# Scales of the MLP weights in four groups, fewer weight tiles asked for in the first units, and four instead of eight float32 units

## The chip, the core and the metric

The kernel runs on one core of one Trainium2 chip. The metric is device time in microseconds (us) of one execution. The five engines of the core have a queue each and run their instructions in the order of that queue: PE (TensorE, matmuls; PEld is its weight load), DVE (VectorE), ACT (ScalarE), POOL (GpSimd) and SP (SyncE, which here issues all DMAs).

## What is computed

Attention in which a query sees only the keys of its own cluster, and behind it an MLP with a squared ReLU:

```python
q_assign = argmax(q_n @ c_n.T); k_assign = argmax(k_n @ c_n.T)     # 16 clusters a head
scores = where(q_assign[:, None] == k_assign[None, :], scale * q @ k.T, -1e9)
attn = exp(scores - max(scores)); attn /= sum(attn) + 1e-9
x = (attn @ v)                                                     # heads side by side: 3072 x 512
h = x @ w_in                                                       # 512 x 2048
g = s * relu(h) ** 2 + b
out = g @ w_out                                                    # 2048 x 512
```

There are 4 batches, 8 heads, 768 positions and a head dimension of 64. The two weight matrices are float64, so a load brings two 32-bit words for each of their elements; the other large inputs are float32.

## The kernel before, in words

**Units.** The attention is cut into 192 units: a batch, one third of its rows (a chunk of 256), a pair of heads, one of two row tiles, one of the two heads. `scores` (L464) makes a unit's 128 x 768 scores on PE into one of two PSUM tiles, `maxima` (L473) takes the row maxima on DVE, `exps` (L480, L483) the exponentials P on ACT. Then P is to be transposed, and there are two ways. The first RAW = 8 units keep P in float32: `low` turns it on PE into the PSUM tile `turned` (L503), DVE and ACT each copy half of it out (helper line L121 for DVE and POOL, L119 for ACT), and `values` multiplies in float32 (L520). The others go in two halves: `high` rounds P to float16 (a copy, on POOL up to unit 18, then on DVE for odd and ACT for even units up to unit 36, then on ACT), POOL subtracts it from P (`low`, L506), SP issues a DMA transpose of both halves (L508), and `values` uses three float16 matmuls for each key tile (L525 to L527). `values` comes five units behind `scores`. `finish_x` collects four units into a slice of x.

**MLP.** From unit LAG = 21 on, each unit is accompanied by one of 192 MLP steps: for a chunk of 256 rows (12 of them) one of the 16 slices of 128 hidden features. `mlp_in` (L583), `mlp_relu` (L590 to L593), POOL's low half (L598), `mlp_out` (L610), which sums over the 16 slices in the PSUM tile `acc` (of which there is one), and an eviction on DVE (L618) at the chunk's end. `mlp_start` (L568 to L574) makes a chunk's scales.

**Weights.** The 32 weight tiles (16 of `w_in`, 16 of `w_out`) stay in SBUF. `weights()` is a generator that for each tile issues its load into one of three `stage` buffers, two tiles later rebuilds a float32 from the two words (`rebase` on ACT, L203; `narrow` on DVE, L207 and L208), and one tile after that takes part in a bound (`bound`: an Abs pass on ACT, L215 and L217; for `w_in` also a sum over rows on PE, L220, and a maximum on DVE, L221). With the last tile `finish_w_in` and `finish_w_out` make one scale for all of `w_in` and one for all of `w_out` (L242 to L257, some 16 small DVE instructions). Only then `wsplit(ft)`, one slice in each unit from 17 to 32, can split the weights into float16 halves (L265 on ACT, L267 on DVE). A split goes into a tile of the pool `w`, which has 33 tiles, so that all but the first use the place of a tile that has just been split. `column_sums` (L275, L278) makes the bias term at the first chunk's end.

**What sets the order.** The main loop asks the generators for one unit after the other: `some(wgen, 2)` at its end asks for two weight tiles in each unit, `background()` moves on the preparation of the coming queries, keys and values (`prep_q`, `prep_k`, `prep_v`, whose start for batch 1 is in START). The framework's scheduler then decides how the instructions of neighbouring units follow each other in each engine's queue; what it wrote is shown under the change.

Of the kernel before, what the change touches and what calls it, by code (L numbers as in the profile page):

```python
# [26 lines left out]
def tile_cluster_attention_mlp(ctx, tc, q, k, v, cent, w_in, w_out, s_in, b_in, out):  # L27
# [18 lines left out]
    RAW = 8  # L46
# [60 lines left out]
    ones = const([P, P], BF16, "ones")  # L107
    G.memset(ones, 1.0)
    ident = const([P, P], F32, "ident")
# [4 lines left out]
    ones16 = const([P, P], F16, "ones16")  # L114
    G.memset(ones16, 1.0)
# [52 lines left out]
    def weight_tile(name):  # L168
        return cp.tile([P, KT, P], F32, tag="w", name=name, bufs=2 * NF + 1)
    w1 = const([P, NF], F32, "w1")  # L170
    l1 = const([P, NF], F32, "l1")
    glob = const([P, 12], F32, "glob")
# [28 lines left out]
    def rebase(d):  # L201
        hw = d["st"][:, :, :, 1].bitcast(F32)
        A.activation(d["w"], hw, AF.Prelu, scale=2.0 ** -112, alpha=-(2.0 ** 32))  # L203

    def narrow(d):
        c = d["w"].bitcast(I32)
        V.tensor_scalar(c, c, 3, None, op0=ALU.logical_shift_left)  # L207
        V.scalar_tensor_tensor(c.bitcast(U32), d["st"][:, :, :, 0].bitcast(U32), 29, c.bitcast(U32),  # L208
                               op0=ALU.logical_shift_right, op1=ALU.bitwise_or)

    def bound(d):
        w, p, ft = d["w"], d["p"], d["ft"]
        wa = sb.tile([P, KT, P], BF16, tag="wab", name=f"wab_{p}", bufs=2)
        if p % 2:
            A.activation(wa, w, AF.Abs, accum_out=l1[:, ft : ft + 1])  # L215
        else:
            A.activation(wa, w, AF.Abs)  # L217
            pw = ps_h.tile([P, 512], F32, tag="h", name=f"pw_{ft}")
            for t in range(KT):
                nc.tensor.matmul(pw[:, :P], ones, wa[:, t, :], start=(t == 0), stop=(t == KT - 1))  # L220
            V.tensor_reduce(w1[:, ft : ft + 1], pw[:, :P], axis=AX.X, op=ALU.max)  # L221
        if ft == NF - 1:
            (finish_w_out if p % 2 else finish_w_in)()
# [3 lines left out]
    def weights():  # L227
        live = {}
        for i in range(2 * NF + 3):
            if 0 <= i - 3:  # L230
                bound(live[i - 3])
# [9 lines left out]
    def finish_w_in():  # L241
        V.tensor_reduce(glob[:, 0:1], w1, axis=AX.X, op=ALU.max)  # L242
        V.tensor_scalar(glob[:, 0:1], glob[:, 0:1], 1.02, None, op0=ALU.mult)
        floor2(V, glob[:, 1:2], glob[:, 0:1])
        inverse2(V, glob[:, 2:3], glob[:, 1:2], 0)
        V.tensor_scalar(glob[:, 2:3], glob[:, 2:3], 2.0 ** 13, None, op0=ALU.mult)
        V.tensor_scalar(glob[:, 1:2], glob[:, 1:2], 2.0 ** -7, None, op0=ALU.mult)

    def finish_w_out():
        lc = columns(1, "w")  # L250
        V.tensor_reduce(lc, l1, axis=AX.X, op=ALU.max)
        allmax(glob[:, 4:5], lc, "w")
        floor2(V, glob[:, 4:5], glob[:, 4:5])
        inverse2(V, glob[:, 5:6], glob[:, 4:5], 0)
        V.tensor_scalar(glob[:, 5:6], glob[:, 5:6], 2.0 ** 13, None, op0=ALU.mult)
        V.tensor_scalar(glob[:, 4:5], glob[:, 4:5], 2.0 ** -13, None, op0=ALU.mult)
        V.tensor_tensor(glob[:, 6:7], sv, glob[:, 4:5], op=ALU.mult)  # L257

    def wsplit(ft):
        while narrowed[0] < 2 * NF:  # L260
            next(wgen)
        made = []
        for w, f in ((wi[ft], glob[:, 2:3]), (wo[ft], glob[:, 5:6])):
# [507 lines left out]
```

## Time and profile before

| | |
|---|---|
| median of three runs | 953.16 us (952.39 to 954.72) |
| profiled execution: device time | 953.86 us |
| profiled execution: span from the first to the last instruction | 952.2 us |
| PE busy | 828.6 us (87%) |
| ACT busy | 711.0 us (75%) |
| DVE busy | 626.1 us (66%) |
| POOL busy | 573.0 us (60%) |

How to read it: the profile is of one execution. An engine's busy time is the time in which one of its instructions ran. A row of a group of instructions gives line, engine, operation, output and input with shapes, then the count, behind the first bar the busy time and the mean duration in ns, behind the second the engine's idle time just ahead of them and what ended it. In a row of a stage (from:to in us from the span's start) the numbers are the stage's length, each engine's busy time with its count of instructions, PE's granted clock as a share of full speed, the busy share of the DMA engines (it can pass 1 where transfers overlap) and GB/s. In a timeline row the first number is the start, the second the duration in us.

### The profile page before, as it was taken

What the parts mean: (1) busy time and instruction counts of PE and PEld (TensorE: products, weight loads), DVE (VectorE), ACT (ScalarE), POOL (GpSimd) and SP (SyncE); (2) the same over time, 40 slices, a digit from 0 to 9 for tenths busy, and PEclk for the clock granted to TensorE, in tenths of its full rate; (3) what the DMA queues carried; (4) which work ended last, traced back from release to release, by engine and by line L of the source; (5) the groups of instructions that cost most, each with busy time, mean ns of one, the idle gap of its engine ahead of it and who ended that gap; (6) DMA issues with size and microseconds to landing.
All of it is one profiled execution on the core that took longest, in us unless ns stands there. A gap on an engine that the chain in (4) does not pass through costs nothing. (4 is left out here: it accounts for less than half of the span.)

```text
span 952.2 us, 22467 instructions
## 1 busy us (share of the span) xinstructions
PE 828.6 (87%) x8625; PEld 579.4 (61%) x8625; DVE 626.1 (66%) x1400; ACT 711.0 (75%) x1390; POOL 573.0 (60%) x596
## 2 busy tenths in 40 slices
PE   0668446988999989999899999999999999999997
PEld 0457324555666667766566666766666766767764
DVE  7797988999677657767865757668666466463100
ACT  4477656887688778987787877978787888789443
POOL 3012545677578566866767758667776765676321
PEclk9965556999999999999999999999999999999999
DMA  6888974876887796968689969758877757777100
GB/s 182 227 215 234 235 179 92 197 151 114 174 167 154 170 201 122 186 147 181 139 165 177 184 142 181 149 130 189 156 153 170 145 116 152 138 165 133 33 23 22
DMA packets 450300, 147.36 MB, mean 155 GB/s; under 512 B 417937, under 2 KB 446609, under 8 KB 450193
## 3 DMA queue, kind: packets, MB, share of 16 engines
q1 hardware_dynamic: 450192, 145.93, 72.2%
q8 instruction: 67, 1.10, 0.5%
q14 instruction: 41, 0.33, 0.1%
HBM read 35.69 MB, written 6.29 MB: 44 GB/s over the span
## 5 line engine op out<-in xcount | busy, mean ns | idle before, releaser
L506 POOL TENSOR_TENSOR ph<-p,ph 128x768 f16<-128x768 f32 x184 | 312.2, 1697 | 123.7 <-ACT ph L119 76.2
L583 PE MATMUL h<-x,wis 128*128 128x256 f16 x2304 | 287.6, 274 | 9.6 <-ACT r L590 8.0
L610 PE MATMUL acc<-wos,g 128*128 128x512 f16 x1152 | 292.6, 379 | 3.2 <-POOL g L598 2.8
L583 PEld LDWEIGHTS <-wis 128*128 128x128 f16 x2304 | 222.2, 98 | 59.5 <-issue 11.3
L598 POOL TENSOR_TENSOR g<-r,g 128x256 f16<-128x256 f32 x192 | 136.6, 713 | 101.7 <-ACT r L593 97.1
L473 DVE TENSOR_REDUCE ssm<-sc 128x1 f32<-128x768 f32 x192 | 181.5, 951 | 24.4 <-PE sc L464 23.6
L483 ACT ACTIVATE p<-sc,ssm,qsm 128x768 f32<-128x768 f32 x192 | 187.7, 978 | 3.4 <-DMA PT<-ph 1.0
L610 PEld LDWEIGHTS <-g 128*128 128x128 f16 x1152 | 103.6, 97 | 87.8 <-POOL g L598 5.7
L480 ACT ACTIVATE ssm<-ssm,lift,qsm 128x1 f32<-128x1 f32 x192 | 73.1, 381 | 92.5 <-DVE ssm L473 91.7
L119 ACT ACTIVATE ph<-p 128x768 f16<-128x768 f32 x164 | 136.1, 830 | 5.8 <-DMA PT<-ph 4.3
L590 ACT ACTIVATE r<-h,cf 128x256 f32<-128x256 f32 x192 | 89.1, 464 | 56.9 <-PE h L583 49.6
L525 PE MATMUL px<-vh,PT 128*128 128x65 f16 x1104 | 120.4, 197 | 12.9 <-DVE xs L537 6.8
L464 PE MATMUL sc<-KA,QA 128*128 128x384 f16 x384 | 99.9, 343 | 26.4 <-ACT p L483 23.4
L526 PE MATMUL px<-vl,PT 128*128 128x64 f16 x1104 | 120.3, 194 | 0.0
L527 PE MATMUL px<-vh,PT 128*128 128x65 f16 x1104 | 120.0, 195 | 0.0
L525 PEld LDWEIGHTS <-PT 128*128 128x128 f16 x1104 | 103.6, 98 | 23.1 <-issue 14.4
L526 PEld LDWEIGHTS <-PT 128*128 128x128 f16 x1104 | 103.3, 100 | 13.2 <-issue 5.1
L464 PE MATMUL sc<-KB,QB 128*128 128x384 f16 x384 | 100.1, 345 | 7.0 <-DMA QB<-qb 7.0
L527 PEld LDWEIGHTS <-PT 128*128 128x128 f16 x1104 | 103.5, 98 | 2.7
L592 ACT ACTIVATE g<-r 128x256 f16<-128x256 f32 x192 | 79.3, 413 | 4.0
L593 ACT ACTIVATE r<-r 128x256 f32<-128x256 f32 x192 | 78.8, 411 | 3.3
L464 PEld LDWEIGHTS <-QA 128*128 128x128 f16 x384 | 35.9, 101 | 54.9 <-issue 29.2
(156 smaller groups left out, 1032.3 us busy)
## 6 DMA issues: line engine op xcount, KB each, us to landing
wst<-in_moe_w_in_dram SPq DMA_DIRECT2D x16, 512.0 KB, 4.5
wst<-in_moe_w_out_dram SPq DMA_DIRECT2D x16, 512.0 KB, 4.5
kn<-in_k_dram SPq DMA_DIRECT2D x16, 384.0 KB, 4.1
qn<-in_q_dram SPq DMA_DIRECT2D x24, 256.0 KB, 3.5
vn<-in_v_dram SPq DMA_DIRECT2D x16, 384.0 KB, 4.1
out_dram<-o SPq DMA_DIRECT2D x12, 512.0 KB, 3.8
PT<-ph SPq DMA_TRANSPOSE x184, 3.5
x<-xn SPq DMA_TRANSPOSE x48, 2.5
```

The source lines that it names most:

```text
L119: A.activation(dst, src, AF.Copy)
L464: last_score[0] = nc.tensor.matmul(sc[:, e, :HALF], X[:, col, :], y[:, h * S + e * HALF : h * S + (e + 1) * HALF], start=st, stop=not st)
L473: last_max[0] = V.tensor_reduce(SM[i // 4][:, 0, j : j + 1], U[i]["sc"], axis=AX.XY, op=ALU.max, negate=True)
L483: last_exp[0] = A.activation(p.rearrange("p (a b) -> p a b", a=2), u["sc"], AF.Exp, bias=bi, scale=u["scale"], **total)
L506: G.tensor_tensor(u["ph"][:, 1, :], u["p"], u["ph"][:, 0, :], op=ALU.subtract)
L525: nc.tensor.matmul(o1, PT[:, kt, :], vh[:, h, kt, : D + 1], start=(kt == 0), stop=False)
L526: nc.tensor.matmul(o, PT[:, kt, :], vl[:, h, kt, :], start=False, stop=False)
L527: nc.tensor.matmul(o1, PT[:, T + kt, :], vh[:, h, kt, : D + 1], start=False, stop=(kt == T - 1))
L583: nc.tensor.matmul(ph[:, :CW], WSP[ft][0][:, wl, kt, :], XS[(b, c, kt)][:, :, xl, :], start=(i == 0), stop=(i == len(terms) - 1))
L590: A.activation(r, ph[:, :CW], AF.Relu, scale=MS[(b, c)][0])
L598: G.tensor_tensor(g[:, 1, :], r, g[:, 0, :], op=ALU.subtract)
L610: nc.tensor.matmul(acc[:, t, :], g[:, gl, rows], WSP[ft][1][:, wl, :], start=(ft == 0 and gl + wl == 0), stop=(ft == NF - 1 and gl == 1))
```

## The change

1. *Groups.* The 16 slices form four groups of four, each with scales of its own (`finish_group`), made as soon as the group's eight tiles are there. The bound is another one: the sums of squares of each column, as the diagonal of a product of the tile with itself on PE (the upper half of each float32 read as bfloat16), four tiles to a PSUM bank and one maximum on DVE for the four; the Abs pass is gone. `wsplit` waits for its group only. In the first chunk each group has its own `mlp_start` and its own accumulation, which DVE scales and adds up; the later chunks go on with one accumulation over all 16 slices, with a factor for each group. The column sums are made by group.
2. *Narrowing.* The shift of the rebuilt word goes into DVE's one remaining instruction (L211 in the new numbering); the low word is brought into place by a second ACT instruction in `rebase`.
3. *Rate.* No weight tile is asked for in units 0 to 3, one in each unit from 4 to 19, two from 20 on. The pool of weight tiles has 35.
4. *Units.* RAW is 4: units 4 to 7 go in two halves. POOL makes the float16 copy up to unit 30.
5. Batch 1's preparation starts at other units, `prep_v(0)` is moved on once more in unit 2, and two constant tiles are made later or not at all.

```diff
-    RAW = 8
+    RAW = 4
...
-        return cp.tile([P, KT, P], F32, tag="w", name=name, bufs=2 * NF + 1)
+        return cp.tile([P, KT, P], F32, tag="w", name=name, bufs=2 * NF + 3)
+    GROUP = 4
+    NG = NF // GROUP
...
     def rebase(d):
         hw = d["st"][:, :, :, 1].bitcast(F32)
         A.activation(d["w"], hw, AF.Prelu, scale=2.0 ** -112, alpha=-(2.0 ** 32))
+        A.activation(d["st"][:, :, :, 0], d["st"][:, :, :, 0].bitcast(U32), AF.Copy, scale=0.9375 * 2.0 ** -29, bias=-0.03125)
 
     def narrow(d):
         c = d["w"].bitcast(I32)
-        V.tensor_scalar(c, c, 3, None, op0=ALU.logical_shift_left)
-        V.scalar_tensor_tensor(c.bitcast(U32), d["st"][:, :, :, 0].bitcast(U32), 29, c.bitcast(U32),
-                               op0=ALU.logical_shift_right, op1=ALU.bitwise_or)
+        V.scalar_tensor_tensor(c.bitcast(U32), c.bitcast(U32), 3, d["st"][:, :, :, 0].bitcast(U32),
+                               op0=ALU.logical_shift_left, op1=ALU.bitwise_or)
...
+    def bound(pairs):
+        pw = ps_h.tile([P, 512], F32, tag="h", name=f"pw_{pairs[0][0]['ft']}")
+        for j, d in enumerate(sum(pairs, [])):
+            wa = d["w"].bitcast(BF16).rearrange("p a (f z) -> p a f z", z=2)[:, :, :, 1]
+            for t in range(KT):
+                nc.tensor.matmul(pw[:, j * P : (j + 1) * P], wa[:, t, :], wa[:, t, :], start=(t == 0), stop=(t == KT - 1))
+        ft = pairs[0][0]["ft"]
+        V.tensor_reduce(wsq[:, ft : ft + 2, :], pw.rearrange("p (f e q) -> p f e q", e=2, q=P), axis=AX.X, op=ALU.max)
+        if (ft + 2) % GROUP == 0:
+            finish_group(ft // GROUP)
...
     def wsplit(ft):
-        while narrowed[0] < 2 * NF:
-            next(wgen)
+        k = ft // GROUP
+        while narrowed[0] < 2 * GROUP * (k + 1):
+            next(wgen, None)
...
-    START = {b: [48 * b + x for x in ((-26, -25, -23, -20) if b == 1 else (-40, -38, -32, -28))] for b in range(1, B)}
+    START = {b: [48 * b + x for x in ((-24, -20, -22, -14) if b == 1 else (-40, -38, -32, -28))] for b in range(1, B)}
...
-        copy(G if i < LAG - 2 else V if i < LAG + NF and i % 2 else A, u["ph"][:, 0, :], u["p"])
+        copy(G if i < LAG + 10 else V if i < LAG + NF and i % 2 else A, u["ph"][:, 0, :], u["p"])
...
+        first = b + c == 0
+        span = GROUP if first else NF
+        k = ft // GROUP
+        if ft % span == 0:
+            MS[(b, c)][2] = ps_a.tile([P, CT, DM], F32, tag="acc", name=f"acc_{n}_{ft}")
...
+                if k == 0:
+                    V.tensor_scalar(o[:, t, :], acc[:, t, :], e, None, op0=ALU.mult)
+                else:
+                    V.scalar_tensor_tensor(o[:, t, :], acc[:, t, :], e, o[:, t, :], op0=ALU.mult, op1=ALU.add)
...
-        some(wgen, 2)
+        some(wgen, 0 if i < 4 else 1 if i < 20 else 2)
```

How the queues change, at three places. DVE before, from the maximum of unit 10 on; `wi` and `wo` are weight tiles, `wst` the loaded words, `pw` the bound's PSUM tile:

```order
L473 TENSOR_REDUCE ssm_864<-sc_975 128x1
L207 TENSOR_SCALAR wi_740<-wi_740 128x512
L68 TENSOR_SCALAR qsm_1_0_829<-qsm_1_0_829 128x2
L221 TENSOR_REDUCE w_128<-pw_774 128x1
L208 SCALAR_TENSOR_TENSOR wi_740<-wst_741,wi_740 128x512
L69 TENSOR_SCALAR qsm_1_0_829<-qsm_1_0_829 128x2
L207 TENSOR_SCALAR wo_783<-wo_783 128x512
L70 TENSOR_SCALAR qsm_1_0_829<-qsm_1_0_829 128x2
L208 SCALAR_TENSOR_TENSOR wo_783<-wst_784,wo_783 128x512
```

DVE in the changed kernel, from the maximum of unit 11 on:

```order
L493 TENSOR_REDUCE ssm_721<-sc_845 128x1
L553 TENSOR_SCALAR ssm_553<-px_859 128x2
L554 RECIPROCAL ssm_553<-ssm_553 128x2
L557 TENSOR_TENSOR xs_796<-px_859,ssm_553 128x128
L105 TENSOR_REDUCE xm_686<-xs_796 128x1
L211 SCALAR_TENSOR_TENSOR wo_740<-wo_740,wst_741 128x512
L221 TENSOR_REDUCE wsq<-pw_906 128x4
L493 TENSOR_REDUCE ssm_965<-sc_958 128x1
```

Of several tiles and two instructions a tile between two maxima one instruction is left, and a maximum over four tiles at once. Ahead of the maximum of unit 21 the changed row holds 19 of the 32 narrowings (three of them ahead of unit 0), the row before all 32.

The second place is DVE at units 26 to 28. Before, `vm` and `qsm` being the next values' and queries' preparation:

```order
L473 TENSOR_REDUCE ssm_1825<-sc_1867 128x1
L98 TENSOR_REDUCE qsm_2_0_1797<-am_q_2_0_1852 128x2
L473 TENSOR_REDUCE ssm_1825<-sc_1968 128x1
L267 SCALAR_TENSOR_TENSOR wos_1964<-wo_783,glob,wos_1964 128x512
L68 TENSOR_SCALAR qsm_2_0_1797<-qsm_2_0_1797 128x2
L101 TENSOR_REDUCE vm_1803<-vn_0_1804 128x1
L69 TENSOR_SCALAR qsm_2_0_1797<-qsm_2_0_1797 128x2
```

The changed kernel there, `gl` and `gsq` being a group's scales and `amb_w` their way to PE:

```order
L493 TENSOR_REDUCE ssm_1827<-sc_2014 128x1
L246 TENSOR_REDUCE amb_w_1780<-wsq 128x2
L282 SCALAR_TENSOR_TENSOR wos_1860<-wo_1090,gl,wos_1860 128x512
L282 SCALAR_TENSOR_TENSOR wis_1867<-wi_1174,gl,wis_1867 128x512
L211 SCALAR_TENSOR_TENSOR wo_1759<-wo_1759,wst_1760 128x512
L102 TENSOR_REDUCE gsq<-am_w_1782 128x2
L248 TENSOR_SCALAR gl<-gsq 128x1
L249 TENSOR_SCALAR gl<-gsq 128x1
L252 TENSOR_SCALAR gl<-gl 128x1 x2
L253 TENSOR_SCALAR gl<-gl 128x1 x2
L60 TENSOR_SCALAR gl<-gl 128x1
```

Narrowings and a group's chain of scales now stand between the splits and the maxima of units 21 to 31.

The third place is SP's queue in the units around 8. Before, loads of weight tiles nearly alone:

```order
L85 DMA wst_784<-in_moe_w_out_dram 128x1024
L85 DMA wst_792<-in_moe_w_in_dram 128x4x256
L85 DMA wst_849<-in_moe_w_out_dram 128x1024
L85 DMA wst_857<-in_moe_w_in_dram 128x4x256
L85 DMA wst_901<-in_moe_w_out_dram 128x1024
L85 DMA wst_909<-in_moe_w_in_dram 128x4x256
L508 DMA_TRANSPOSE PT_923<-ph_916 128x12x128
```

The changed kernel, one load for each transpose of P:

```order
L528 DMA_TRANSPOSE PT_660<-ph_653 128x12x128
L89 DMA wst_712<-in_moe_w_in_dram 128x4x256
L528 DMA_TRANSPOSE PT_727<-ph_719 128x12x128
L89 DMA wst_741<-in_moe_w_out_dram 128x1024
L528 DMA_TRANSPOSE PT_755<-ph_748 128x12x128
L89 DMA wst_816<-in_moe_w_in_dram 128x4x256
```

The transposes of units 4 to 8 have taken places between the loads, and the later loads have moved back past the transposes of later units.

More of the change, by code (lines that the diff above doesn't have):

```diff
@@ L106, in tile_cluster_attention_mlp @@
         G.memset(rev[:, c : c + 1], float(C - c))
-    ones = const([P, P], BF16, "ones")
-    G.memset(ones, 1.0)
-    ident = const([P, P], F32, "ident")
+    ident = sb.tile([P, P], F32, tag="g", name="ident", bufs=4)
     G.memset(ident, 1.0)
@@ L229, in weights @@
         for i in range(2 * NF + 3):
-            if 0 <= i - 3:
-                bound(live[i - 3])
+            p = i - 3
+            if p >= 0 and p % 4 == 3:
+                bound([[live[p - 3], live[p - 2]], [live[p - 1], live[p]]])
+            if p >= 0:
                 narrowed[0] += 1
@@ L602, in mlp_out @@
         n = f"{b}_{c}"
-        if ft == 0:
-            MS[(b, c)][2] = ps_a.tile([P, CT, DM], F32, tag="acc", name=f"acc_{n}")
+        first = b + c == 0
+        span = GROUP if first else NF
+        k = ft // GROUP
+        if ft % span == 0:
+            MS[(b, c)][2] = ps_a.tile([P, CT, DM], F32, tag="acc", name=f"acc_{n}_{ft}")
         acc = MS[(b, c)][2]
@@ L608, in mlp_out @@
             rows = slice(t * P, t * P + P)
-            for gl, wl in ((0, 0), (0, 1), (1, 0)):
-                nc.tensor.matmul(acc[:, t, :], g[:, gl, rows], WSP[ft][1][:, wl, :],
-                                 start=(ft == 0 and gl + wl == 0), stop=(ft == NF - 1 and gl == 1))
-        if ft == NF - 1:
-            _, e, acc = MS.pop((b, c))
-            o = sb.tile([P, CT, DM], F32, tag="stage", name=f"o_{n}", bufs=3)
-            if b + c == 0:
+            for gi, wl in ((0, 0), (0, 1), (1, 0)):
+                nc.tensor.matmul(acc[:, t, :], g[:, gi, rows], WSP[ft][1][:, wl, :],
+                                 start=(ft % span == 0 and gi + wl == 0), stop=(ft % span == span - 1 and gi == 1))
+        if ft % span < span - 1:
+            return
+        e = MS[(b, c)][1][:, k : k + 1] if first else MS[(b, c)][1][:, 0:1]
+        if k == 0 or not first:
+            MS[(b, c)].append(sb.tile([P, CT, DM], F32, tag="stage", name=f"o_{n}", bufs=3))
+        o = MS[(b, c)][3]
+        if first:
+            if ft == NF - 1:
                 column_sums()
             for t in range(CT):
+                if k == 0:
+                    V.tensor_scalar(o[:, t, :], acc[:, t, :], e, None, op0=ALU.mult)
+                else:
+                    V.scalar_tensor_tensor(o[:, t, :], acc[:, t, :], e, o[:, t, :], op0=ALU.mult, op1=ALU.add)
+                if ft == NF - 1:
+                    V.tensor_tensor(o[:, t, :], o[:, t, :], bias[0], op=ALU.add)
+        else:
+            for t in range(CT):
                 V.scalar_tensor_tensor(o[:, t, :], acc[:, t, :], e, bias[0], op0=ALU.mult, op1=ALU.add)
+        if ft == NF - 1:
+            MS.pop((b, c))
             nc.sync.dma_start(out[b * S : (b + 1) * S].rearrange("(p t) e -> p t e", t=T)[:, c * CT : (c + 1) * CT, :], o)
@@ L674, in prepare @@
                 run(first_k[3])
-                some(first_v, 1)
+                some(first_v, 2)
             if k == 3:
```

116 lines of the change are left out of this document (64 added, 52 removed).

## The prediction

> **What bounds the kernel now.** I read the page first: the span and the forty slices.
>
> ```profile
> span 952.2 us, 22467 instructions
> PE   0668446988999989999899999999999999999997
> DVE  7797988999677657767865757668666466463100
> PEclk9965556999999999999999999999999999999999
> DMA  6888974876887796968689969758877757777100
> ```
>
> From the tenth slice on (about 235 us) PE is full in almost every slice. Before it PE is half empty, its clock is at 5 tenths for a while, and DVE and the DMA engines carry the high digits. The change edits only things that happen before that point, so I cut the span at the row maxima of certain units (L473 on DVE, one per unit): unit 0 begins at 34.85 us, unit 8 at 70.84, unit 21 at 149.54, unit 32 at 210.66 and unit 42 at 262.22; the last exponential is at 878. Each engine's busy time by stage:
>
> ```profile
> core 0: us, PE busy (x) PEld busy (x) DVE busy (x) ACT busy (x) POOL busy (x), PEclk, DMA share, GB/s
> 34.85:70.84 35.99, 26.18 (x188) 20.16 (x187) 31.02 (x69) 26.02 (x54) 4.29 (x6) 0.77 0.90 239
> 70.84:149.54 78.70, 46.97 (x342) 33.32 (x339) 66.68 (x137) 49.77 (x97) 35.37 (x30) 0.59 0.80 200
> 149.54:210.66 61.12, 50.35 (x528) 34.42 (x529) 55.59 (x104) 48.00 (x92) 39.37 (x34) 0.89 0.77 159
> 210.66:262.22 51.56, 46.31 (x472) 30.16 (x470) 41.09 (x95) 36.56 (x68) 32.65 (x30) 1.00 0.73 147
> 262.22:878.00 615.78, 583.54 (x6472) 410.94 (x6470) 396.95 (x887) 502.89 (x979) 431.12 (x425) 1.00 0.78 158
> ```
>
> I call the first two rows stage A (units 0 to 20, 114.7 us), the third B (units 21 to 31, 61.1), the fourth C, the fifth D. In D, PE is busy 583.5 of 615.8 us (95%): nothing but PE work matters there, and the change leaves D's work alone. In B, DVE is busy 55.6 of 61.1 (91%): it is the bound. In A, DVE is busy 97.7 of 114.7 (85%) with the DMA engines close behind. So the question is what moves out of A, what moves into B, and at what rate each gives or takes.
>
> **What leaves A.** These are the DVE groups of stage A, by shape:
>
> ```profile
> L473 DVE TENSOR_REDUCE ssm<-sc 128x1 f32<-128x768 f32 x21 | 19.9, 950 | 4.0 <-PE sc L464 4.0
> L208 DVE SCALAR_TENSOR_TENSOR wi<-wst,wi 128x512 uint32<-128x512 uint32 x14 | 14.7, 1048 | 0.1
> L208 DVE SCALAR_TENSOR_TENSOR wo<-wst,wo 128x512 uint32<-128x512 uint32 x15 | 12.7, 850 | 0.1
> L207 DVE TENSOR_SCALAR wi<-wi 128x512 int32<-128x512 int32 x14 | 9.6, 689 | 3.7 <-ACT wi L203 3.7
> L207 DVE TENSOR_SCALAR wo<-wo 128x512 int32<-128x512 int32 x15 | 6.9, 457 | 4.0 <-ACT wo L203 4.0
> L121 DVE COPY PT<-turned 128x384 f32<-128x384 f32 x8 | 4.4, 547 | 1.8 <-PE turned L503 1.8
> L221 DVE TENSOR_REDUCE w<-pw 128x1 f32<-128x128 f32 x15 | 4.2, 281 | 1.4 <-PE pw L220 1.4
> L101 DVE TENSOR_REDUCE amb_q<-qn 128x2 bf16<-128x512 f32 x2 | 1.4, 686 | 1.3 <-DMA qn<-in_q_dram 1.3
> ```
>
> Twenty-nine of the 32 weight tiles are narrowed in A now. In the changed program's written-out row on DVE 16 of these come ahead of the maximum of unit 21, and 13 behind it. So, on DVE in A:
> - L208: 27.4 us for 29 tiles, 16 stay: -12.3. The new instruction has the same two inputs and shape, so I keep its price.
> - L207 is folded into it: -16.5.
> - L221: -4.2, and in its place four reductions of 128x512, which I price as the one of the same length, amb_q, at 0.69: +2.7.
> - Four copies of turned P, at 0.547: -2.2.
> - The single scale chain, some 16 small instructions, becomes the first group's, 24 small ones. The small ones are in this excerpt of DVE's timeline:
>
> ```profile
> 132.10 0.15 DVE L243 TENSOR_SCALAR glob<-glob 128x1 f32<-128x1 f32 x1
> 132.84 0.15 DVE L246 TENSOR_SCALAR glob<-glob 128x1 f32<-128x1 f32 x1
> 132.91 0.14 DVE L247 TENSOR_SCALAR glob<-glob 128x1 f32<-128x1 f32 x1
> ```
>
> They take 0.15 each (0.07 from start to start where the next doesn't wait for the one before): 24 x 0.15 - 2.9 = +0.7.
>
> Sum on DVE: -31.8, from 97.7 to 65.9 us. At A's present 85% that would be 77.5 us, but another cover comes up first, the DMA engines. They are busy 0.90 x 36.0 + 0.80 x 78.7 = 95.4 us of A. One weight tile costs 1.92 us of them: 0.524 MB at 298 GB/s is 1.76, times the share of 1.09 in this window:
>
> ```profile
> 36.00:48.00 12.00, 10.32 (x77) 8.00 (x78) 7.99 (x16) 8.52 (x20) 0.59 (x1) 1.00 1.09 298
> ```
>
> Thirteen tiles fewer are -25.0. The four units that leave the float32 way add four transposes of 0.393 MB; at D's 158 GB/s for a share of 0.78, one is 1.94: +7.8. That leaves 78.2 us. I take 84 us for A (93% of that share; DVE at 78%), so **A: -31**. The lower end is 78 (the share goes to 1 and beyond, as in the row above): -37. The upper end is 98, if only half of DVE's relief is turned into time: -17.
>
> What also eases A: ACT and PE.
>
> ```profile
> L203 ACT ACTIVATE wo<-wst 128x512 f32<-128x512 f32 x15 | 9.9, 661 | 7.0 <-DMA wst<-in_moe_w_out_dram 7.0
> L215 ACT ACTIVATE wab<-wo 128x512 bf16<-128x512 f32 x15 | 9.4, 625 | 2.6 <-DVE wo L208 2.5
> L520 PE MATMUL px<-vn,PT 128*128 128x64 f32 x96 | 20.0, 386 | 0.0
> L503 PE MATMUL turned<-ident,p 128*128 128x128 f32 x48 | 12.3, 385 | 7.2 <-DVE PT L121 3.7 <-ACT p L483 2.1 <-ACT PT L119 1.3
> ```
>
> The Abs pass (0.625) goes and a conversion of the low words comes; its shape and stride are L203's, so 0.66: a wash per tile, never on the path at ACT's 66% in A. The exponentials stand behind L203 in ACT's queue, and L203 waits 7.0 us there for tiles that have just been asked for; with one tile per unit the tile has landed long before. The float32 way costs PE 4.0 us per unit (20.0 / 8 + 12.3 / 8), so four units fewer are 16 us of PE, in a stage where PE holds up the scores behind it. On the other side, POOL gets four casts and four subtractions:
>
> ```profile
> L506 POOL TENSOR_TENSOR ph<-p,ph 128x768 f16<-128x768 f32 x11 | 19.3, 1751 | 0.6
> L121 POOL CAST ph<-p 128x768 f16<-128x768 f32 x11 | 11.3, 1024 | 18.6 <-ACT p L483 16.6 <-issue 2.0
> ```
>
> That is 2.8 us for each pair, so POOL goes from 39.7 us to 51 of 84, no bound.
>
> **What enters B.** DVE's groups in B, and the eviction's row from C:
>
> ```profile
> L267 DVE SCALAR_TENSOR_TENSOR wis<-wi,glob,wis 128x512 f16<-128x512 f32 x11 | 12.9, 1168 | 0.7 <-ACT wis L265 0.7
> L267 DVE SCALAR_TENSOR_TENSOR wos<-wo,glob,wos 128x512 f16<-128x512 f32 x12 | 11.3, 943 | 1.4 <-ACT wos L265 1.3
> L473 DVE TENSOR_REDUCE ssm<-sc 128x1 f32<-128x768 f32 x11 | 10.4, 947 | 0.6 <-PE sc L464 0.5
> L121 DVE CAST ph<-p 128x768 f16<-128x768 f32 x6 | 3.8, 630 | 0.0
> L618 DVE SCALAR_TENSOR_TENSOR o<-acc,xm,bias 128x512 f32<-128x512 f32 x2 | 1.4, 746 | 0.0
> ```
>
> Thirteen narrowings at 0.95 (the mean of L208's 29): +12.3. Four reductions at 0.69: +2.7. Three chains of scales, 72 small instructions at 0.15: +10.8. Three more starts of the first MLP chunk, 21 small ones at 0.17: +3.5. Two group evictions of the accumulator, four at 0.75: +3.0. Six casts move to POOL: -3.8. Sum +28.5, from 55.6 to 84.1 us. B is DVE's already, so nothing hides this; the only give is DVE's idle 9%. Some of that closes, because ACT and DVE now pass one spare tile to and fro:
>
> ```profile
> ACT wis L265 <- DVE wos L267: 9.1, 5, 2.6
> ACT wos L265 <- DVE wis L267: 5.9, 7, 1.7
> ```
>
> With two tiles more, ACT's 15 us of waiting for L267 can run ahead. I take 95.5% for DVE: 84.1 / 0.955 = 88.1, **B: +27**. Lower end: narrowing at its undisturbed 0.68 (below) and small ones at 0.10: -7, so +20. Upper end: 91% as now and PE's slower clock (second rival): +39.
>
> The price of 0.95 holds POOL's interference, seen where both engines' rows stand together (start, duration):
>
> ```profile
> 121.79 1.63 POOL L506 TENSOR_TENSOR ph<-p,ph 128x768 f16<-128x768 f32 x1
> 121.82 2.15 DVE L208 SCALAR_TENSOR_TENSOR wi<-wst,wi 128x512 uint32<-128x512 uint32 x1
> ```
>
> The weight tile's own view gives L208's least, median and greatest duration in ns:
>
> ```profile
> L208 DVE SCALAR_TENSOR_TENSOR wi<-wst,wi x16: 676/692/2152, 26.4 to 127.1; 128x512 uint32<-128x512 uint32 x16
> ```
>
> L208's minimum is 0.68; started 0.03 us behind a POOL subtraction of 1.63, it took 2.15, about the two in a row. Eleven casts more on POOL in B (units 19 to 30 no longer use DVE or ACT for them) make this likelier. [...]
>
> **C to the end.** The first chunk's accumulator is now read in four parts and the column sums in four, each time with PE waiting for a DVE instruction of 0.75: four such waits in C, about 1.2 us each with the wait for DVE's turn, +5. The splits that C still does now are done in B, and C's PE is busy 46.3 of 51.6, so some of that idle time closes: -3. **C: +2** (-4 to +6). D and the tail keep their instructions: 0.
>
> Sum: -31 + 27 + 2 = -2 us against the profiled execution's 953.9 us, which lies 0.7 above the median of the three runs (953.2). So 951 for the median. DVE's total is nearly the same before and after (about -31.8 + 28.5 and a little in C): work is moved, not saved, and a gain needs A to shrink by more than B grows.
>
> **The rivals.**
> 1. *Faster.* A goes to its DMA floor of 78 us (-37) and B takes only its lower +20, since narrowing loses the instruction (L207) that POOL stretched to 689 ns in the mean against 457 for the other half, and ACT runs ahead. -37 + 20 + 2 = -15: 938. For it: A's idle times are waits of weights on DMA and of scores on float32 PE work, both of which go. Against it: the 12.3 us of narrowing meet POOL in B as well.
> 2. *Slower, PE's clock.* PE's granted clock follows its busy share in the stage rows: 60% busy has 0.59, 82% has 0.89, 90% has 1.00. B stretched to 88 us holds 50.4 us of PE plus some 6 for 64 squaring matmuls (four in 0.40 us at full clock, below): 64%, near A's. If the clock falls to 0.6, PE's 44.8 + 6 us at full clock become 85, as much as DVE's 84, and each then waits for the other in queue order: B at about 100, +39. -31 + 39 + 2 = +10: 963. It decides from a clock under 0.7 in B; above that PE has room. The matmuls priced here, from the timeline:
>
> ```profile
> 45.37 0.40 PE L220 MATMUL pw<-wab,ones 128*128 128x128 bf16 x4
> ```
>
> [...]
> 3. *Slower, A does not shrink.* The change's first aim fails: the transposes of units 4 to 7 and weight tiles queue behind each other on SP, which issues in order, and A stays at 98. -17 + 27 + 2 = +12: 965.
>
> **How the numbers follow.** Cancelling within a few us (944 to 958): 0.40, of which 0.17 under 950.3, 0.17 within, 0.06 above. Rival 1: 0.27. Rival 2: 0.25. Rival 3: 0.08. About 0.3% (2.9 us, 950.3 to 956.0) is what a measurement of this kernel can tell from no change. Faster: 0.17 + 0.27 = 0.44; same: 0.17, with 0.01 from the upper rivals' lower edge, 0.18; slower: 0.06 + 0.33 - 0.01 = 0.38. The range reaches from rival 1's 938 with 3 us of its own spread to rival 3's 965 with 3: 935 to 968; the likeliest case's own is 944 to 958.
>
> **What would show it.** The maximum of unit 21 near 119 us (A at 84), with the DMA share above 0.9 in A; the maximum of unit 32 near 207, with DVE busy over 90% between the two; PE full from there. Unit 21 before 115 and unit 32 before 200 is rival 1. A granted clock under 0.7 and PE busy over 85% between units 21 and 32 is rival 2. Unit 21 after 130 is rival 3. The forecast is wrong altogether if stage D's 615.8 us change by more than a few us, since I give no reason for that.

## The result: 3.4% slower, and where the profile after shows it

| | before | after |
|---|---|---|
| median, four runs each, on one chip by turns | 953.94 us (952.39 to 957.18) | 986.92 us (984.81 to 989.29) |
| ratio, 95% interval | | 1.0342 [1.0303, 1.0381] |
| profiled execution, span | 952.2 us | 986.2 us |

The forecast was 951 us, and its range ended at 968. These are the same rows of the page of after, and below them the stages cut at the same maxima (L493 on DVE now), with a stretch further on. One limit in the prediction is misnamed: counted by their records, the maximum that begins at 262.22 us in before is the 44th, so unit 43's and not unit 42's; in after the 44th begins at 283.31.

```profile
span 986.2 us, 22636 instructions
...
PE   0585566598998799999889889999889899999997
...
DVE  6767598999477666637746557656656556464100
...
PEclk9956579899999799999999999999999999999999
DMA  6869899579669896996799898979779778878300
```

The stages of after (columns as in the prediction):

```profile
35.65:76.41 40.76, 30.35 (x229) 23.57 (x228) 29.18 (x59) 20.20 (x36) 16.22 (x15) 0.75 0.82 165
76.41:135.85 59.44, 32.78 (x306) 21.18 (x306) 40.77 (x100) 36.34 (x63) 34.52 (x30) 0.63 0.93 205
135.85:221.60 85.75, 61.62 (x609) 40.93 (x609) 77.92 (x214) 63.21 (x121) 48.13 (x45) 0.88 0.81 189
...
308.00:333.00 25.00, 15.93 (x189) 10.05 (x186) 19.71 (x42) 14.56 (x24) 15.49 (x14) 0.74 0.84 170
```

Stage A went from 114.7 to 100.2 us (-14.5; forecast -31), B from 61.1 to 85.8 (+24.6; forecast +27), C, up to 283.31, from 51.6 to 61.7 (+10.1; forecast +2). The last exponential came at 878 before and at 911.9 now, so D went from 615.8 to 628.6 (+12.8; forecast 0). The last row above is a hole: around 320 us, far behind all weights, PE is busy 15.93 of 25 us and its clock falls to 0.74. The same stretch of before has none:

```profile
308.00:333.00 25.00, 24.07 (x271) 17.11 (x269) 15.98 (x40) 18.71 (x37) 15.12 (x15) 1.00 0.81 176
```

Stages cut by units hide one thing: MLP steps shift among them. A better ledger is PE's unused time. Busy time multiplied by the granted clock is PE's work, in us at full clock; the length of a stretch less this work is what PE left unused, by idling or by a low clock. It is summed over stretches of 5 us (192 such rows for before, 201 for after). "MLP step 40" is the start of that step's relu on ACT (345.1, 364.7 and, in the run with both mends told below, 354.4 us).

| PE time not used, us | before | after | both mends |
|---|---|---|---|
| up to unit 0 | 28.1 | 29.4 | 30.3 |
| A: units 0 to 20 | 66.8 | 58.7 | 55.3 |
| B: units 21 to 31 | 14.8 | 31.2 | 31.2 |
| unit 32 to MLP step 40 | 11.4 | 20.4 | 13.4 |
| MLP step 40 to the last exponential | 26.2 | 39.3 | 23.6 |
| tail | 5.8 | 6.0 | 6.3 |
| sum | 153.1 | 185.0 | 160.1 |
| span less sum: PE's work | 799.1 | 801.2 | 798.6 |

PE's work is nearly the same in sum (799 to 801 us): the float32 work that went has been made up by work that came, the squares among it. So a shorter A is worth only what it takes from PE's unused time, and that is 8 us, not 14.5. B loses 16 again, and 22 us are lost behind unit 32, where the forecast had 2.

The start of some MLP steps (their relu on ACT) shows the same as differences to before, in us; one_sum to before_shift160 are runs told below:

| MLP step (before at) | after | one_sum | align | one_align | before_shift160 |
|---|---|---|---|---|---|
| 8 (195.5) | +9.7 | +7.7 | +8.4 | +7.6 | +0.9 |
| 28 (295.0) | +0.5 | +10.6 | -0.7 | +4.9 | +4.3 |
| 32 (314.0) | +18.2 | +17.7 | +16.5 | +11.9 | +6.1 |
| 40 (345.1) | +19.5 | +15.8 | +16.9 | +9.2 | +6.4 |
| 88 (548.3) | +27.3 | +22.6 | +17.0 | +8.0 | +13.5 |
| 188 (936.1) | +33.8 | +24.1 | +15.6 | +6.0 | +18.3 |

At step 28 after stands level with before. That is not the whole state of the kernel: at step 8 it was 9.7 us behind, and its attention is 11 us behind at the maximum of unit 32 (221.60 against 210.66) and 21 us at the 44th (283.31 against 262.22). Behind step 28 come a step of 18 us and a drift of 14.

**The step.** DVE's timeline of after holds the four readings of the column sums (start, duration):

```profile
254.51 0.74 DVE L296 TENSOR_SCALAR bias<-pb,gl 128x512 f32<-128x512 f32 x1
...
258.80 0.75 DVE L298 SCALAR_TENSOR_TENSOR bias<-pb,gl,bias 128x512 f32<-128x512 f32 x1 [2.68 <-PE pb L293]
...
263.78 0.75 DVE L298 SCALAR_TENSOR_TENSOR bias<-pb,gl,bias 128x512 f32<-128x512 f32 x1 [3.37 <-PE pb L293]
...
268.11 0.75 DVE L298 SCALAR_TENSOR_TENSOR bias<-pb,gl,bias 128x512 f32<-128x512 f32 x1 [3.58 <-PE pb L293]
```

ACT's timeline there has the exponentials of units 40 and 41, next to each other in its row of exponentials, and further on the relu of MLP step 32:

```profile
254.37 0.97 ACT L503 ACTIVATE p<-sc,ssm,qsm 128x768 f32<-128x768 f32 x1
...
278.72 0.97 ACT L503 ACTIVATE p<-sc,ssm,qsm 128x768 f32<-128x768 f32 x1
...
332.24 0.47 ACT L617 ACTIVATE r<-h,cf 128x256 f32<-128x256 f32 x1 [1.54 <-DVE cf L600]
```

And PE's has the last of the four sums and the first matmul of the values behind it:

```profile
266.18 1.89 PE L293 MATMUL pb<-wos,ones 128*128 128x512 f16 x8
...
272.31 0.19 PE L545 MATMUL px<-vh,PT 128*128 128x65 f16 x1
```

The four sums go through the one PSUM tile `m`, which the values need too. Between two sums PE's row has an MLP step, so the tile is held until 268.9 us, the values come at 272.3, and the next exponential is 24.4 us behind the last. (That it waits for the values because they give P's buffers back is read from the program; the trace lists no wait for it.) Between the same two exponentials lie 7.7 us in before, 17.5 in before with four sums, 9.5 in after with one sum: the gap comes and goes with the sums. PE is full meanwhile (busy in all 24.35 us from 254.37 to 278.72), with MLP steps. But these run out: step 32 is the first of a chunk whose x the late units still have to make, and its relu waits until 332.24 for `cf`, the chunk's scale. In the hole itself PE waits 3.7 us for one exponential and 2.9 us for the next queries (QA). How far the scores are ahead of the MLP stands in PE's written-out row (units whose scores come before the step's first matmul, less the step's number):

| MLP step | 16 | 20 | 24 | 28 | 32 | 36 |
|---|---|---|---|---|---|---|
| before | 21 | 23 | 22 | 23 | 23 | 23 |
| after | 21 | 23 | 19 | 18 | 18 | 23 |
| after with one sum | 21 | 22 | 22 | 22 | 22 | 23 |
| before with four sums | 21 | 23 | 20 | 21 | 21 | 22 |

**The drift.** This is the stretch from MLP step 40 to the last exponential, in before:

```profile
345.10:878.00 532.90, 506.77 (x5611) 357.25 (x5608) 340.31 (x771) 434.01 (x846) 370.68 (x364) 1.00 0.77 156
```

In after:

```profile
364.70:911.90 547.20, 512.39 (x5605) 358.16 (x5602) 331.88 (x770) 435.83 (x847) 369.75 (x366) 0.99 0.85 152
```

In before with its buffers shifted (before_shift160, below):

```profile
351.60:896.30 544.70, 508.36 (x5608) 356.73 (x5605) 335.83 (x769) 434.35 (x846) 370.02 (x364) 1.00 0.84 153
```

In after with both mends (one_align, below):

```profile
354.40:884.00 529.60, 506.02 (x5609) 357.16 (x5606) 340.26 (x772) 435.65 (x848) 372.13 (x367) 1.00 0.79 157
```

It is the same work, and from unit 100 on PE's instructions stand in the same order before and after. But after's DMA engines are busy 0.85 of the time for 152 GB/s, against 0.77 for 156. The transposes themselves are slower. The trace records every single DMA packet, and those of 256 bytes are the transposes' (in before there are 406016, just as many as its transposes fill by their shapes). Between 500 and 850 us such a packet takes 21.2 ns in the mean in before and 24.4 in after, one of 4096 bytes 174 and 176. The page's row of the transposes of P, with the median us from issue to landing, before:

```profile
PT<-ph SPq DMA_TRANSPOSE x184, 3.5
```

And after:

```profile
PT<-ph SPq DMA_TRANSPOSE x188, 4.0
```

PE's waits for the turned queries, another transpose, from 345 us on (us in total, times, longest), before:

```profile
PE pq L395 <- DMA QA<-qa: 1.5, 2, 1.0
```

And after:

```profile
PE pq L415 <- DMA QA<-qa: 4.1, 4, 2.2
```

What differs is where the buffers lie. In the program before, the large ones (P, its halves, the turned halves; 3072 bytes each in a partition) begin at byte 107008, a multiple of 512; in the changed one at 114336, 160 bytes past one. The constants that the change removes and adds, two weight tiles and an identity that now lies in another pool shift everything behind them by 7328 bytes, which is 160 more than a multiple of 512.

### The profile page after: what moved, and what is told of

Its sections match the earlier page's. It is cut to its first block, busy times and chain, and to the rows that moved or that the text cites. A ratio compares the mean times of both kernels' runs of the same rounds, so it can differ in the third digit from the quotient of the medians.

```text
span 986.2 us, 22636 instructions
## 1 busy us (share of the span) xinstructions
PE 838.6 (85%) x8696; PEld 579.5 (59%) x8696; DVE 608.8 (62%) x1464; ACT 705.0 (71%) x1359; POOL 589.4 (60%) x615
## 5 line engine op out<-in xcount | busy, mean ns | idle before, releaser
L526 POOL TENSOR_TENSOR ph<-p,ph 128x768 f16<-128x768 f32 x188 | 318.0, 1691 | 111.2 <-ACT ph L119 73.4
L610 PE MATMUL h<-x,wis 128*128 128x256 f16 x2304 | 291.9, 276 | 12.8 <-ACT r L617 7.8
L610 PEld LDWEIGHTS <-wis 128*128 128x128 f16 x2304 | 224.6, 99 | 65.2 <-issue 16.9
L625 POOL TENSOR_TENSOR g<-r,g 128x256 f16<-128x256 f32 x192 | 134.2, 700 | 128.4 <-ACT r L620 118.9
L493 DVE TENSOR_REDUCE ssm<-sc 128x1 f32<-128x768 f32 x192 | 181.6, 951 | 40.1 <-PE sc L484 39.4
L545 PE MATMUL px<-vh,PT 128*128 128x65 f16 x1128 | 124.9, 198 | 13.3 <-DVE xs L557 8.9
L119 ACT ACTIVATE ph<-p 128x768 f16<-128x768 f32 x158 | 131.2, 830 | 6.6 <-DMA PT<-ph 5.7
L546 PE MATMUL px<-vl,PT 128*128 128x64 f16 x1128 | 124.9, 195 | 0.0
L547 PE MATMUL px<-vh,PT 128*128 128x65 f16 x1128 | 124.7, 196 | 0.0
L545 PEld LDWEIGHTS <-PT 128*128 128x128 f16 x1128 | 107.5, 99 | 24.8 <-issue 16.4
L546 PEld LDWEIGHTS <-PT 128*128 128x128 f16 x1128 | 107.2, 101 | 14.7 <-issue 6.8
L547 PEld LDWEIGHTS <-PT 128*128 128x128 f16 x1128 | 107.3, 99 | 2.2
```

The lines of the kernel that those rows point to most:

```text
L119: A.activation(dst, src, AF.Copy)
L493: last_max[0] = V.tensor_reduce(SM[i // 4][:, 0, j : j + 1], U[i]["sc"], axis=AX.XY, op=ALU.max, negate=True)
L526: G.tensor_tensor(u["ph"][:, 1, :], u["p"], u["ph"][:, 0, :], op=ALU.subtract)
L545: nc.tensor.matmul(o1, PT[:, kt, :], vh[:, h, kt, : D + 1], start=(kt == 0), stop=False)
L546: nc.tensor.matmul(o, PT[:, kt, :], vl[:, h, kt, :], start=False, stop=False)
L547: nc.tensor.matmul(o1, PT[:, T + kt, :], vh[:, h, kt, : D + 1], start=False, stop=(kt == T - 1))
```

## The experiments

Times are medians; a ratio is to the kernel before, run by turns on the same chip, with its 95% interval.

**One accumulation for the column sums** (on after)

```diff
-        for k in range(NG):
-            pb = ps_m.tile([P, 512], F32, tag="m", name=f"pb{k}")
...
+        ones16 = const([P, NG], F16, "ones16")
+        V.tensor_scalar(ones16, gl[:, 4, :], gl[:, 5, 0:1], None, op0=ALU.mult)
+        pb = ps_m.tile([P, 512], F32, tag="m", name="pb")
...
+            one = ones16[:, j // (2 * GROUP) : j // (2 * GROUP) + 1].broadcast_to([P, P])
+            nc.tensor.matmul(pb, one, WSP[j // 2][1][:, j % 2, :], start=(j == 0), stop=(j == n - 1))
```

> The changed kernel with the column sums of w_out made in one accumulation again (the factor of each group, a power of four, is put into the ones that multiply, so the result is the same) instead of four accumulations with a DVE reading behind each. Theory S (the four sums hold the one PSUM tile m from 252 to 272 us, the values and with them the row tiles and the exponentials stand still, PE runs six MLP steps ahead, and at MLP step 32 the MLP has to wait for x): the step of 18 us between MLP steps 28 and 32 goes, in PE's row the scores stay 22 units ahead of the MLP instead of falling to 18, and the time is 966 to 970 us if the later drift of 15 us has another cause, 950 to 956 if it is the same. Theory P (the later preparation of batch 1 is what holds up the attention): the step stays, 980 to 988. Theory R (four instead of eight float32 units and the shifted weights leave everything behind): the step stays, 980 to 988.

979.23 us, ratio 1.0249 [1.0216, 1.0281]. The hole fills:

```profile
308.00:333.00 25.00, 21.31 (x266) 14.78 (x263) 15.87 (x41) 17.09 (x33) 16.26 (x17) 1.00 0.92 154
```

The time gains 7.7 us, not 18, and misses the 966 to 970 that theory S gave: without the lump of sums the MLP is 10 us later at step 28 already (table above). A part of the step was a loan, MLP work that had been done early. At step 32 itself one_sum is only 0.5 us ahead of after (+17.7 against +18.2); its gain appears behind that step, up to 9.7 us at step 188. With aligned buffers (align against one_align, below) 4.6 us of it are there at step 32 and 7.7 at step 40. So the sums cost time, but the step at 32 is not theirs alone, and the cost that theory S gave them was put too high.

**Batch 1's preparation at the old units** (on after)

```diff
-    START = {b: [48 * b + x for x in ((-24, -20, -22, -14) if b == 1 else (-40, -38, -32, -28))] for b in range(1, B)}
+    START = {b: [48 * b + x for x in ((-26, -25, -23, -20) if b == 1 else (-40, -38, -32, -28))] for b in range(1, B)}
```

> The changed kernel with batch 1's preparation started at the units of before (-26, -25, -23, -20 for -24, -20, -22, -14). Theory S: the four column sums stay, the step of 18 us at MLP step 32 stays, 982 to 990. Theory P: the step goes, 966 to 972. Theory R: 982 to 990.

998.39 us, 1.0445 [1.0403, 1.0487], above all three ranges. Theory P falls: the later start is no cause of the loss, and the old one costs 11 us more here; why, no run asks.

**Four column sums in the kernel before**

```diff
+        for k in range(4):
+            pb = ps_m.tile([P, 512], F32, tag="m", name=f"pb{k}")
+            for j in range(8):
+                nc.tensor.matmul(pb, ones16, WSP[4 * k + j // 2][1][:, j % 2, :], start=(j == 0), stop=(j == 7))
...
+                V.scalar_tensor_tensor(bias[0], pb, glob[:, 7:8], bias[0], op0=ALU.mult, op1=ALU.add)
```

> The kernel before with its column sums in four accumulations, each read by DVE, as in the change; everything else as before. Theory S: the scores' lead in PE's row falls from 23 to 20 or 21 (in the changed kernel to 18), so part of the step comes: MLP step 32 is 4 to 12 us later than before, 957 to 967. Theories P and R: within 2 us of before, 952 to 956.

962.42 us, 1.0075 [1.0047, 1.0103], MLP step 32 at 321.0 us (+6.9). So the four sums alone cost some 7 us, in either kernel (here by the ratio).

**Eight float32 units** (on after: `RAW = 8`)

> The changed kernel with eight float32 units again. Theory S: the step at MLP step 32 stays; PE has some 10 us more work (16 us of float32 work in, 6 of float16 out), 985 to 1000. Theory P: the same. Theory R: the step gets smaller, 965 to 980.

1004.13 us, 1.0502 [1.0457, 1.0548], 4 us above the range of theory S. Theory R falls: the time did not come down with the eight float32 units.

**Where the buffers lie.** Three kernels; the first moves the 160 bytes of scales behind the large buffers, the second puts 160 unused bytes ahead of the buffers of before, the third is one_sum and align together.

```diff
-    gl = const([P, 10, NG], F32, "gl")
...
+    gl = sb.tile([P, 10, NG], F32, tag="gl", name="gl", bufs=1)
```

```diff
+    pad = const([P, 40], F32, "pad")
+    G.memset(pad, 0.0)
     rev = const([P, C], F32, "rev")
```

> The changed kernel with its small tile of scales (160 bytes) allotted behind the large buffers instead of ahead of them, so that the buffers of P, its halves and the turned halves begin at multiples of 512 bytes again, as before (114176; in the changed kernel 114336, which is 160 past one). All instructions stay the same and in the same order. Theory L (the layout slows the DMA transposes: in stage D they take 84 to 85% of the DMA engines for the same bytes against 76% before, PT lands after 4.0 us against 3.5, and the small stalls of PE follow): the share goes back to 75 to 78%, the drift of some 15 us behind MLP step 32 goes for the greater part, 970 to 979. Theory O (the drift comes from how the engines' phases stand to each other): the share and the time stay, 983 to 990.

> The kernel before with an unused constant of 160 bytes ahead of everything, so that its buffers lie as the changed kernel's do (the large ones 160 bytes past a multiple of 512, KA and QA at 64, x at 288). Nothing else differs but one memset on POOL at the start. Theory L: the DMA share in stage D goes from 76 to 84%, and the time grows by 8 to 16 us, to 962 to 972. Theory O: within 2 us of before, 952 to 957.

> Both mends on the changed kernel: the column sums in one accumulation, and the large buffers at multiples of 512 bytes. Theory L together with theory S (four sums): 979 less 8 to 15, 963 to 971. Theory O: 977 to 982, as with the one sum alone.

align: 972.16 us, 1.0175 [1.0146, 1.0204], 14.8 less than after. before_shift160: 973.15 us, 1.0187 [1.0154, 1.0219]: 17 us from 160 bytes that nothing reads. one_align: 963.71 us, 1.0085 [1.0052, 1.0119]. Theory L is shown in both directions (before_shift160 is 1 us above its range), and the two causes add up: 14.8 and 7.7 are 22.5, and one_align lies 23.2 below after. The ratios, each to before on the same chip, say the same: 0.0167 and 0.0093 are 0.0260, against 0.0257. Two more pads asked how far off is too far:

> The kernel before with 256 unused bytes ahead of everything: the large buffers then begin 256 bytes past a multiple of 512. In the runs so far, 160 and 192 past cost the DMA engines 83 to 85% of stage D, 0 past 76 to 77%. If what counts is a multiple of 256 or less, 76% and 952 to 957; if it is 512, 82 to 85% and 962 to 973.

> The kernel before with 128 unused bytes ahead of everything, the large buffers at 128 bytes past a multiple of 512. If a multiple of 128 is enough: 76% of the DMA engines in stage D and 952 to 958; if 256 is needed: 82 to 85% and 963 to 974.

256 bytes: 955.61 us, 1.0005 [0.9986, 1.0023]. 128 bytes: 970.45 us, 1.0153 [1.0113, 1.0193]. The queue's row between 500 and 850 us (packets, MB, share of the DMA engines), for 256 bytes:

```profile
q1 hardware_dynamic: 189953, 53.83, 75.2%
```

And for 128 bytes:

```profile
q1 hardware_dynamic: 185026, 52.59, 82.1%
```

So of the five offsets tried, 0 and 256 bytes past a multiple of 512 cost nothing that can be measured, and 128, 160 and 192 (the buffers in one_sum: ratio 1.0249, against 1.0085 in one_align) do: the two that cost nothing are the multiples of 256. The 256-byte packets say it too: 20.7 ns at 256, 21.2 at 0 (before, and align as well), 23.7 at 128, 23.8 at 192, 24.0 at 160 in before_shift160 and 24.4 in after, while those of 4096 bytes stay at 170 to 178 in all of them. The share of the DMA engines goes with the offset as well (75.2% at 256, 82.1% at 128). Why such an offset makes a packet slower, no run shows; whether the reads or the writes of the transposes pay, and in which of the buffers, is not separated by these runs, as every pad moves all that lies behind it.

**What holds stage A.** Squares in bursts behind the scores, on after:

```diff
+            with behind(last_score[0]):
                 for t in range(KT):
                     nc.tensor.matmul(pw[:, j * P : (j + 1) * P], wa[:, t, :], wa[:, t, :], start=(t == 0), stop=(t == KT - 1))
```

> The changed kernel with the squaring matmuls of the bound ordered behind the scores of the unit that asks for them, so that they come in PE's row in bursts of four tiles each fourth unit, on tiles that are ready, and not one tile in each unit ahead of the next scores. Theory Q (in units 9 to 20 PE waits 17 us for DVE's narrowing, the scores stand behind the squares, and so A takes 100 us instead of 84): the maximum of unit 21 comes 8 to 15 us earlier, at 121 to 128 us, and the time falls by as much as B and C do not eat, 974 to 984. Theory F (A is at the floor of its DMA engines, which are busy 0.89 of it): unit 21 stays within 3 us of 135.85, 984 to 990.

989.62 us, 1.0379 [1.0336, 1.0422], unit 21 at 135.2 us. Theory Q falls: the 17 us that PE waits for narrowed tiles were not what set A. PE's waits in units 8 to 20, in after:

```profile
PE pw L219 <- DVE wi L211: 8.6, 4, 3.3
PE pw L219 <- DVE wo L211: 8.5, 5, 3.2
PE sc L484 <- ACT p L503: 2.2, 2, 2.0
```

With the squares in bursts PE waits as long, for the exponentials instead:

```profile
PE sc L485 <- ACT p L504: 14.0, 6, 5.6
PE pw L220 <- DVE wo L211: 3.2, 3, 1.3
```

Then the weight loads free of their place behind the transposes on SP, on one_align (`load(..., src, True)`), and more of them early (`1 if i < 12 else 2`, and one in every unit):

> The changed kernel with both mends, and the weight loads no longer ordered on SP behind the last transpose. Theory T (in units 9 to 20 each weight load stands on SP behind a transpose that waits for POOL's subtraction, lands late, and holds up ACT, which stands on it with the next exponential behind; 12.6 of 60 us): the loads go out ahead, the maximum of unit 21 comes before 128 us, and the total falls by some of it, 952 to 961. Rival (the loads then crowd the first units as before, and A is as long): 962 to 972.

> The changed kernel with both mends (963.7), and two weight tiles asked for in each unit from 12 on instead of from 20 on: eight tiles move from B into A. Theory B (the rest of the loss is DVE's load in units 21 to 31, 78 of 86 us): B gets 6 to 9 us shorter, A 0 to 3 longer as DVE has 30% to spare there, 956 to 960. Theory F (A stands at its DMA engines, 0.9 busy, some 1.9 us a tile): A gets 10 to 15 us longer, 965 to 972.

> The changed kernel with both mends, and one weight tile asked for in every unit from 0 on to the end, never two: four tiles more come ahead of unit 4, and behind unit 20 the tiles come one by one. Theory B: the lumps of DVE in units 25 to 31 get smaller, 956 to 961. Theory F: the first units get 4 to 8 us longer and nothing is gained, 963 to 970.

974.16 us (1.0187 [1.0148, 1.0227]; unit 21 at 148.3 us), 981.87 (1.0275 [1.0215, 1.0334]; 140.7) and 972.28 (1.0192 [1.0153, 1.0231]; 136.6), against 134.0 for unit 21 in one_align. All three are slower than any of their expectations gave. Loads that come earlier make A longer, by 5 to 10 us. That it is because A stands at its DMA engines (theory F) does not follow: in oneal_free A is the longest, 107.7 us, and they are busy 0.76 of it, against 0.87 in one_align. Stage B of one_align and then of oneal_rate12:

```profile
134.00:219.70 85.70, 62.43 (x607) 41.11 (x607) 77.91 (x214) 62.38 (x120) 47.95 (x45) 0.86 0.80 187
140.80:225.30 84.50, 65.39 (x644) 45.23 (x643) 68.62 (x188) 61.37 (x119) 43.78 (x46) 0.87 0.59 138
```

B is only 1.2 us shorter, though DVE's busy time there falls from 77.9 to 68.6 us. So DVE's load alone does not set B either. In oneal_rateall B is 12.6 us shorter (73.1), with 17 us less for DVE to do; but from unit 32 to the 44th maximum it takes 72.2 us, against 53.0 in one_align. And parts 2 and 4 alone, on the kernel before:

> The kernel before with only part 2 of the change: the shift of the high word goes into DVE's one remaining instruction and ACT brings the low word into place; layout, order of the weights, float32 units and scales as before. If DVE (85% busy) is what holds units 0 to 20, 16.5 us of it go and the maximum of unit 21 comes 8 to 16 us earlier, 941 to 949; if ACT's 19 us more of work or the waits between engines hold them, within 3 us of before, 952 to 959.

> The kernel before with only part 4 of the change: four float32 units instead of eight (and the preparation of v moved on once more in unit 2, without which unit 4 would have no split v); copies, weights, scales and layout as before. If four float32 units fewer are worth what PE's ledger says (8 us of PE work less, in a stretch in which PE waits as well), 943 to 950; if the weights of 24 tiles still hold that stretch, within 3 us of before, 952 to 958.

> The kernel before with part 2 (narrowing in one DVE instruction) and four float32 units together, nothing else: the parts of the change that take work away, without the four groups of scales, the later weights and the shifted buffers. If DVE and PE together hold the first units: 938 to 948. If each of them only uncovers the next wait there: 952 to 958.

959.46 us (1.0050 [1.0027, 1.0073]; unit 21 at 156.0 against 149.5), 956.81 (1.0014 [1.0002, 1.0027]) and 959.03 (1.0038 [1.0020, 1.0057]). None of the three brings a gain. Stage A of before_narrow:

```profile
34.60:156.10 121.50, 74.39 (x528) 54.58 (x526) 86.84 (x176) 89.92 (x179) 40.77 (x36) 0.61 0.80 201
```

DVE has 10.9 us less to do in A than before (86.84 for 97.7), ACT 14.1 more (89.92 for 75.8), and A is 6.8 us longer. So A does not follow DVE's load alone. What relief of DVE would give with no more work for ACT, no run shows: in this one the gain can have been lost on ACT.

**Two smaller undoings**, on one_align: POOL's extra casts (the old rule of the copy) and the old narrowing.

> The changed kernel with both mends (one sum, aligned buffers; 963.7) and the old rule for the float16 copy (POOL up to unit 18, then DVE and ACT by turns) instead of POOL up to unit 30. Theory C (POOL's casts and subtractions hold DVE's two-input instructions up in units 21 to 31: the split of w_out took 1293 ns in the mean there, against 943 before): those splits go back to about 950 ns, stage B gets 3 to 6 us shorter, 957 to 961. Rival (DVE has as much more to do by taking six casts of 0.63 us itself): 962 to 967.

> The changed kernel with both mends (963.7) and the old narrowing, two DVE instructions for each tile and one ACT instruction, instead of one and two. If what part 2 cost the kernel before (4 us) is also its cost here: 958 to 961. If DVE's load in units 21 to 31 counts for more (15 tiles by 0.57 us are 8.6): 966 to 973.

962.10 us (1.0070 [1.0049, 1.0090]) and 967.67 (1.0129 [1.0096, 1.0161]). Without POOL's casts the split of w_out takes 919 ns in B, against 1208 in one_align (1293 in after), but a narrowing takes 880 for 733, and DVE does the six casts itself. B is 3.7 us shorter (82.1 for 85.8), the stretch from unit 32 to the 44th maximum 8.2 longer, and in the whole time the intervals show no difference to one_align. The old narrowing is 4 us slower here than the new, with intervals that overlap: part 2 is no cause of what is left. It gives DVE 8.7 us more in B (86.7 for 78.0), and B is 8.3 us longer (94.1): there DVE's load does count.

## Why the prediction was wrong, point by point

- **A, -31.** It came to -14.5: this step failed as well as the one on D below. The work on DVE was near (65.9 forecast, 69.95 measured), though one reading under it was off: in the trace 14 narrowings of after stand in A and 15 behind the maximum of unit 21, not 16 and 13, so 17 and not 19 are ahead of that maximum. The consequence was wrong. DVE is busy 70% of A now, not 78 or 85, and in before_narrow less work on DVE made A no shorter. The DMA floor of 78.2 us was too low: 0.82 x 40.8 + 0.93 x 59.4 = 88.7 us, of which aligned buffers take back little (0.87 of 97.5 us in one_align). And ACT's waits for loaded words, which were to go with one tile in each unit, stayed. ACT's waits in A, in before and, below the dots, in after:

```profile
ACT wo L203 <- DMA wst<-in_moe_w_out_dram: 7.0, 7, 1.9
ACT wi L203 <- DMA wst<-in_moe_w_in_dram: 5.6, 6, 1.4
...
ACT wo L206 <- DMA wst<-in_moe_w_out_dram: 10.1, 7, 3.6
ACT wi L206 <- DMA wst<-in_moe_w_in_dram: 1.6, 2, 1.1
```

  A at 100.2 is near what rival 3 said (98), and its sign came, unit 21 after 130 us. Its mechanism, SP's order, is not borne out: with the loads freed from it ACT waits 17.4 us for them in A, and A gets longer. Which of the waits between ACT, DVE, PE and the DMA engines sets A stays open.
- **B, +27.** Right in size: +24.6, with DVE busy 77.92 of 85.75 us (91%; forecast 84.1 of 88.1). Part of that is luck: DVE got 22.3 us more to do and not 28.5, though 15 narrowings came and not 13 (at 0.77 us each, not 0.95), and the share at which DVE was to run, 95.5%, stayed at 91. Rival 2's clock under 0.7 did not come: 0.88. With POOL's casts one of DVE's two-input instructions takes longer (the split of w_out, 1208 ns in one_align and 919 without them in oneal_copy) and another does not (a narrowing, 733 and 880), and in the whole time they cost nothing that can be measured.
- **C, +2.** The mechanism was named, the size not: "four such waits in C, about 1.2 us each" priced the waits of PE and of DVE's turn. What the four sums hold up is the PSUM tile `m`, and so the values and, 24.4 us apart, the exponentials. C itself got 10.1 us longer, and the four sums cost the kernel 7 to 9 us (before_four, one_sum, align against one_align); in the trace the loss shows some 50 us later, when the MLP steps pulled forward have run out.
- **"D and the tail keep their instructions: 0."** This is the step that failed by a cause of which the text had nothing. The instructions were kept, even in their order; their buffers were not. The allotment moved by 160 bytes off a multiple of 256, and that is 15 to 17 us (align, before_shift160). No rival held it, and the reservation in the text's last sentence had no price. The written-out order cannot show it; the allotment could have been read ahead. Without it the time would still lie outside the range (align, 972.16), as it would without the four sums alone (one_sum, 979.23); without both it lies inside (one_align, 963.71), with A 14 us longer than forecast.
- **Sum.** With both mends the kernel is 0.85% slower than before. By the ledger that is B (+16.4) against A (-11.5) and smaller terms; this is an account of where PE's time goes, not a cause shown by a run. Undoing the copies or the narrowing does not take it away, so what would make B cheaper stays open. No version of the change here beats the kernel before.

## What to carry to other kernels

Where one engine is full for most of the time, keep a ledger of its unused time by stretches, and not of the stages' lengths: a stage can get shorter because its work went elsewhere. A change of any constant moves the buffers behind it (160 bytes did here); read where the buffers of the DMA transposes begin before and after, and keep them at multiples of 256 bytes, the only offsets of the five tried here that cost nothing (ratio 1.0005 with a pad of 256, 1.0153 with one of 128). And an accumulation cut into parts through a single PSUM tile has the price of all who need that tile (7 to 9 us for the four sums here), which is paid where the work that was pulled forward meanwhile runs out.

## What the hardware showed that was not expected

The same transposes, in the same order, took the DMA engines 75 to 79% of a stretch with their buffers at 0 or 256 bytes past a multiple of 512 (75.2% in before_shift256 and 76.1% in before between 500 and 850 us, 79% in align from MLP step 40 to the last exponential), and 82 to 85% at 128 or 160 (82.1% in before_shift128 between 500 and 850 us, 84% in before_shift160 and 85% in after from step 40 on). For the whole kernel before that is 955.6 us with a pad of 256 bytes against 970.5 with one of 128. A 256-byte packet of theirs takes 24 ns (23.7 to 24.4) instead of 21 (20.7 to 21.2). The transposes of P land half a microsecond later (a median of 4.0 us against 3.5), and the kernel before, whose PE is busy 506.77 of 532.90 us (95%) from MLP step 40 to the last exponential, loses 1.5% (before_shift128) to 1.9% (before_shift160) by it.
